# 64-key score blocks in query subgroups of 256, with each chunk's exp split over separate PSUM banks

## The chip, the cores and the metric

The kernel runs on one core of a Trainium2 chip. The metric is the device time of one execution in microseconds (us). A profiled execution also has a span, from its first to its last instruction, which is 1.8 us shorter than the time of the same run (307.76 against 306.0 us before the change). PE is the matmul engine (TensorE) and PEld its weight loads, DVE is VectorE, ACT is ScalarE, POOL is GpSimd.

## The reference, cut to what matters

One transformer block on 2048 tokens of 512 features: adaptive layernorm, sliding-window attention with 32 heads of 16 features, then a token-mixing MLP of width 1792.

```python
mod = (_silu(c) @ w_mod).reshape(c.shape[0], 6, 1, -1)       # six vectors sa, ca, ga, sb, cb, gb
h = _layernorm(x) * (1 + ca) + sa
# attention: 32 heads of 16, window of 256 keys
scores = jnp.einsum('bhqd,bhkd->bhqk', q, k) * Dh ** (-0.5)
mask = (idx[:, None] - idx[None, :] >= 0) & (idx[:, None] - idx[None, :] < 256)
p = _softmax(jnp.where(mask, scores, -1e9))
x = x + ga * (p @ v, heads joined) @ wo
h = _layernorm(x) * (1 + cb) + sb
# MLP over tokens
u = _gelu(jnp.einsum('bsd,sf->bdf', _layernorm(h), w1) + b1)
x = x + gb * (jnp.einsum('bdf,fs->bds', u, w2) + b2)
```

## The kernel before

The 2048 queries go in four groups of 512. Heads go in four sets of eight. Four heads share the PE array by row tiles, and a chunk fills a score tile of four PSUM banks, one bank for each `j`, which one exp reads. The kernel lays out eight PSUM banks: four for the scores (`pss`), one each for value products and sums (`pox`, `poy`), two for everything else (`psd`).

```python
pss = box["s"] = ps_s.tile([P, 4, D], F32, name="pss", tag="pss")      # ps_s has bufs=1
for pi, (kb, q0, nq, at) in enumerate(ch):
    for j in range(4):
        rows = slice(32 * j, 32 * j + 32)
        te.matmul(pss[:, j, HB * at : HB * (at + nq)], lhsT=KT[r][g8][rows, kbi, :, :, :],
                  rhs=QT[G % 2][g8][rows, HB * q0 : HB * (q0 + nq)], start=pi == 0, stop=False, ...)
...
def e_e(e, i=i):
    et_of[i] = epool.tile([P, 4, D], BF, name="et")
    ac.activation(out=et_of[i][:], in_=box["s"][:], func=ACT.Exp, scale=SCORE_SCALE)
```

The chunks called "l" do the half-filled blocks at the window's edges with many small matmuls (64 scores of 32 columns for each of two head sets, four at a time), and DVE multiplies their exps by a mask (`el`). Sums of exps come from a product with a constant `ones_bd`. Their reciprocal is taken on ACT, as `exp(-ln(sum))` (`lz`), and a DVE multiplication writes `OT`. Instructions are issued in a fixed order, kept as a long list of numbers in the source. In it a letter behind a number sends an operation to ACT, DVE or POOL.

The softmax here doesn't subtract the row's maximum and nothing guards it: scores larger than these inputs give would overflow.

Of the kernel before, what the change touches and what calls it, by code (L numbers as in the profile page):

```python
# [10 lines left out]
ALU = mybir.AluOpType  # L11
PSUM = bass.MemoryType.PSUM

P = 128
# [10 lines left out]
HB = 32  # L25
NC = S // NG // HB
# [21 lines left out]
41 30 0 3 42 55 5 49 4 48 13 38 12 54 56 29 1 40 57 78 6 58 2 34 8 37 25 79 53 7 45 15 59 44 80 22 39 9 33 10 81 82  # L48
51 11 46 26 43 83 60 35 20 50 32 16 47 85 84 36 14 61 52 86 28 63 87 18 88 21 89 64 27 90 93 19 92A 91D 94 31 24 96D
95A 17 97 98 100 99A 101 104 102A 103D 105 235 145 107A 112 106D 146 113 115D 108 109 114D 111A 148 62 116 149 110D  # L50
117 123 119D 124 118D 125A 151 152 120 126 121 127 131 122D 132 236 154 133A 134 237 128 155 135 129 238 136 130D
147 163 156 137 164 150 139 157 140 239 166 144 23 153 240 167 138D 158 241 65 242 141D 159 169 66 69 142 170 143 67
70 243 160 175 68 244 176 245 161 73 162 571 403 178 248 179 249 247D 165 246D 168 404 252 251A 250D 181 171 74 182
255 256 253 172 254D 184 173 268 174 185 269 257D 270D 264 259 193 77 177 271D 258 194 186 272 265 196 405 180 197
183 187 273 267D 199 188 200 266D 275D 276 277 274D 189 301 278D 279 302 406 260 261 280 190 304 305 191 281D 192 76
195 263D 283 407 307 262D 198 282 308 292 284 293 294D 310 201 311 285 71 286D 75 202 313 72 203 745 749 295 204 314
748 296 746 752 303 750 205 747 297A 322 315 306 323 206 316 287 288 289A 300 325 207 309 326 408 312 217 291 211
290 572 212 328 409 208 329 410 209 213 317 210 318 218 331 214 332 215 416 216 411 319 337 417 338 320 412 413 418D
321 415D 324 219 414A 340 419D 327 341 220 330 423 333 221 343 420 222 344 424 421 425D 334 422D 346 427 436 347 226
299 428 429 298 437 430D 335 349 223 439A 350 336 438D 339 342 431D 358 224 432 359 345 433 351 447 361 435D 348 362  # L60
353 434D 225 448 354 364 455 449D 365 456 352 440 457D 450 355 367 426 444 368 356 441 451 227 357 458 443D 442A 469
459 228 360 470 363 229 445 573 230 472 366 232 473 231 452 233 369 234 446D 453 370 475 454D 376 371 574 373 476
372 377 575 478 378 374 479 379 380 381 481 375 385 471 482 382 386 383 474 384 490 387 463 491 460 388 483 389 493
464 494 390 461 477 468 576 394 496 480 497 577 485 484 578 486 499 391 500 392 487 505 506 488 393 489 492 465A 395
508 466 495 509 498 396 467 501 397 753 754 502 462D 511 398 512 580 399 402 401 400 579 755 503 514 756 504 515 581
757D 507 583D 584 585 582D 517 587D 586D 591 518 592 596 597 593A 599D 526 510 527 595 598D 588 594 589 600 590D 529
519 513 530 601 608 609 516 603A 610D 532 602D 521 533 611D 612 613 520 758 522 535 614D 523 759 760 536 761 764
762D 765 524 766 637 525 638 528 604 605 640 606D 767 641 607D 531 534 768D 537 643 538 620 644 621 615 622D 616 769
539 617D 646 540 619 770 647 541 618 771 542 772 649 773D 774 543 639 650 553 623 624 547 625D 548 658 549 642 659
651 544 631 545 652 661 632 662 546 645 633D 550 551 554 634 664 552 626 628 665 629 555 627 648 636 763 635 775 556  # L70
630A 667 653 668 776 780 777 654 781 655 673 778 674 656 782 657 660 557 676 779A 558 663 677 783 786 785 784D 787
751 562 788 679 559 666 680 669 791 560 792 789 670 682 790A 561 793 683 797 798 794 799 796 671 685 795A 672 800
686 675 801D 678 563 802 694 564 803 695 808 565 804 809 687 805 566 697 681 806D 698 684 568 689 570 569 688 813
690 700 691 814 815 701 692 810 567 816 811 703 693 704 696 699 702 812A 705 817D 819 706 830 833 820 832 707 821
842 822 835 708 709 818 823D 844 710 836 712 711 713 721 715 716 714 722 717 718 869 729 824 825 875 723 719 733 845
724 846 720 870 734 876 725 826 881 741 726 730 827 828A 829 831 727 887 839 857 840 735 863 728 838 851 807 731 888
736 837 852 834 882 841 742 843 864 737 883 877 732 738 858 889 871 739 847 859 743 740 865 853 744 848 854 849 878
860 850 855 866 856 861 890 884 862 867 872 893 868 873 911 874 879 905 917 885 912 894 886 891 918 880 899 895 892
900 939 901 896 906 897 923 940 898 913 907 908 929 902 914 903 930 924 909 925 910 915 931 919 904 920 932 921 926
933 927 969 949 928 959 916 979 970 922 934 950 989 999 980 1000 981 982 960 961 990 941 962 942 943 971 972 951 944  # L80
991 935 963 936 945 1001 946 952 953 1009 1019 954 955 964 956 1020 1010 937 965 957 938 1029 1021 947 1002 966 948
1011 1030 983 992 1031 993 1003 973 974 1022 1012 994 984 1039 985 975 995 976 1023 1032 967 1040 977 968 1013 1024
986 978 1033 958 1041 996 1014 1004 1005 1034 1006 1042 1035 987 1043 1007 1015 1049 997 1069 1016 998 1050 1008
1070 988 1079 1071 1025 1051 1026 1059 1052 1017 1053 1060 1036 1018 1044 1027 1045 1054 1037 1061 1046 1055 1038
1072 1028 1047 1062 1063 1056 1048 1073 1074 1064 1065 1057 1080 1066 1058 1075 1081 1076 1082 1083 1077 1084 1067
1085 1078 1086 1068 1087 1088
# [3 lines left out]
def run_order(ops):  # L90
    engines = {"A": "ACT", "D": "DVE"}
    left = set(range(len(ops)))
    for word in ORDER.split():
        n = int(word.rstrip("AD"))
        o = ops[n]
        if any(d.n in left for d in o.deps):
            raise RuntimeError(o.name)
        left.discard(n)
        o.emit(engines[word[-1]] if word[-1] in engines else next(iter(o.engs)))
    if left:  # L100
        raise RuntimeError(sorted(left))
# [3 lines left out]
E_BUFS = 5  # L105
WARM = 24



CHUNKS = [  # L110
    [(-1, 0, 7, 0), (-4, 0, 1, 7), (7, 15, 1, 8), (4, 9, 7, 9)],
    [(-2, 0, 5, 0), (5, 11, 5, 5), (-3, 0, 3, 10), (6, 13, 3, 13)],
    [(0, 1, 8, 0), (1, 3, 8, 8)],
    [(2, 5, 8, 0), (3, 7, 8, 8)],
]
CHUNK_G0 = [(7, 15, 1, 0), (4, 9, 7, 1), (6, 13, 1, 8), (5, 11, 5, 9), (6, 14, 2, 14)]

EDGES = [
    ((8, 0, 2), (6, 0, 2)),
    ((5, 8, 1), (4, 8, 1)),  # L120
    ((0, 8, 1), (7, 8, 1)),
    ((0, 8, 1), (7, 8, 1)),
]
EDGES_G0 = ((0, 8, 2), None)
NEG = -32768.0
# [3 lines left out]
def kernel(  # L129
# [73 lines left out]
    edge_w = const.tile([P, 2, 2, 2, HB], BF, name="edge_w")  # L203
    edge_n = const.tile([P, 2, 4, HB], BF, name="edge_n")
    maskl = const.tile([P, 2, HB], BF, name="maskl")
    ones_bd = const.tile([P, 2 * DH], BF, name="ones_bd")
    nc.gpsimd.memset(ones_bd[:], 0.0)
    par_of = const.tile([P, 2], F32, name="par_of")
    nc.gpsimd.memset(par_of[:], 0.0)
    for q in range(4):  # L210
        par = q % 2
        rows = slice(HB * q, HB * q + HB)
        nc.gpsimd.memset(ones_bd[rows, par * DH : (par + 1) * DH], ZSCALE)
        nc.gpsimd.memset(par_of[rows, par : par + 1], 1.0)
    half = const.tile([P, 4], F32, name="half")
    for hf in range(2):
        rows = slice(KB * hf, KB * hf + KB)
        nc.gpsimd.memset(half[rows, 0:1], 1.0 - hf)
        nc.gpsimd.memset(half[rows, 1:2], float(hf))
        nc.gpsimd.memset(half[rows, 2:3], hf - 1.0)  # L220
        nc.gpsimd.memset(half[rows, 3:4], -float(hf))
# [8 lines left out]
    KT = [[kvpool.tile([P, 8, 2, 2, HB], BF, name=f"KT{r}_{g}") for g in range(ND)] for r in range(3)]  # L230
# [9 lines left out]
    ps_s = ctx.enter_context(tc.tile_pool(name="ps_s", bufs=1, space=PSUM))  # L240
    ps_o = ctx.enter_context(tc.tile_pool(name="ps_o", bufs=1, space=PSUM))
# [15 lines left out]
    def emit_masks():  # L257
        tri4 = modw.tile([P, 4, HB], BF, name="tri4")
        tri = modw.tile([P, HB], BF, name="tri")
        po.memset(tri4[:], 1.0)  # L260
        po.affine_select(
            out=tri4[:], in_=tri4[:], pattern=[[HB, 4], [1, HB]],
            compare_op=ALU.is_ge, fill=0.0, base=0, channel_multiplier=-1,
        )
        po.memset(edge_w[:], 0.0)
        for q in range(4):
            rows = slice(HB * q, HB * q + HB)
            po.tensor_copy(out=tri[rows, :], in_=tri4[rows, q, :])
# [51 lines left out]
    def e_warm(e):  # L320
        if "warm" not in box:
            box["warm"] = ps_o.tile([P, D], F32, name="pox")
# [767 lines left out]
```

## Time and profile before

| | before |
|---|---|
| median time | 306.6 us (3 runs), 307.8 us (4 runs, with the profiled one) |
| span | 306.0 us |
| PE busy | 263.4 us, 86% |
| DVE busy | 190.9 us, 62% |
| ACT busy | 178.3 us, 58% |
| POOL busy | 29.3 us, 10% |
| head, to the first exp | 22.1 us |
| attention, to the last value matmul | 193.3 us |
| tail (MLP) | 90.6 us |

A busy share is an average over stages that have different limits, so the table is read by its last three rows. The lines behind them stand in the prediction.

### The profile page before, as it was taken

The page shows a single profiled execution, that of the slowest core. Times are in us where ns is not written, and L with a number is a line of the kernel's source. Part 1 is how long each engine was busy: PE and PEld are TensorE (multiplying, and loading weights), DVE is VectorE, ACT ScalarE, POOL GpSimd, SP SyncE. Part 2 cuts the span into 40 slices and gives each one's busy share as a digit, 9 for nine tenths or more (in the row PEclk, how much of TensorE's full clock was granted, in tenths as well). Part 3 has the DMA queues.
Part 4 walks back from the last instruction along what each step waited for, and adds up shares of the span by engine and source line. Part 5 has one row for each costly group of instructions (what it writes and reads, how often), then busy time and mean ns, then how long its engine had stood idle before and what let it go on. Part 6 is the DMA issues. An engine that isn't in the chain of part 4 may idle for free.

```text
span 306.0 us, 12754 instructions
## 1 busy us (share of the span) xinstructions
PE 263.4 (86%) x5961; PEld 148.4 (49%) x5961; DVE 190.9 (62%) x367; ACT 178.3 (58%) x178; POOL 29.3 (10%) x87
## 2 busy tenths in 40 slices
PE   8287988897988878858899989969999999999973
PEld 3154655554455653545566536446443444444431
DVE  5345997856767886988474682755696531144754
ACT  2057787886788799799597669848342722000000
POOL 8101111010102050001100130000000000000000
PEclk9789999999899999999999999999999999999999
DMA  6997000006900000000000410520689600011121
GB/s 122 243 348 253 5 2 4 4 4 181 237 4 4 4 2 5 4 2 4 4 4 4 111 30 4 140 72 2 250 295 372 257 0 0 0 36 52 61 76 51
DMA packets 31453, 24.94 MB, mean 82 GB/s; under 512 B 6056, under 2 KB 29608, under 8 KB 31400
## 3 DMA queue, kind: packets, MB, share of 16 engines
q1 hardware_dynamic: 30336, 23.08, 25.0%
q10 hardware_dynamic: 1064, 1.05, 1.1%
q8 instruction: 46, 0.75, 1.0%
q14 instruction: 7, 0.06, 0.1%
HBM read 22.03 MB, written 2.10 MB: 79 GB/s over the span
## 4 chain that ended last, share of the span: by engine, by line
PE 66%; ACT 20%; issue 5%; DVE 4%; DMA 3%; SPq 1%; ACTq 0%; DVEq 0%
PE pu L169 32%; ACT et L169 18%; PE pss L169 12%; PE pq L169 7%; PE pox L169 5%; PE poy L169 4%; PE pa L169 3%; DMA x<-in_A_x_dram 3%; PE pv L169 2%; SPq L169 1%; DVE o L169 1%; DVE a L169 1%; PE pt L169 1%; ACT h1T L169 1%; PE ps_b L169 1%
## 5 line engine op out<-in xcount | busy, mean ns | idle before, releaser
L169 ACT ACTIVATE et<-pss 128x2048 bf16<-128x2048 f32 x68 | 127.6, 1876 | 33.3 <-PE pss L169 31.7
L169 PE MATMUL pu<-hb,w1p 128*128 128x512 bf16 x224 | 54.4, 380 | 2.7 <-DVE a L169 1.1
L169 PE MATMUL pu<-guT,w 128*128 128x512 bf16 x224 | 50.0, 379 | 2.5 <-DVE o L169 2.5
L169 PE MATMUL pss<-QT,KT 32*64 32x32 bf16 (+5 forms) x1744 | 35.4, 210 | 14.1 <-ACT et L169 10.1
L169 PEld LDWEIGHTS <-KT 32*64 32x64 bf16 (+1 forms) x1744 | 22.9, 98 | 37.0 <-issue 34.7
L169 POOL TENSOR_SCALAR KT<-kb,mask_par 128x512 bf16<-128x512 bf16 x30 | 21.6, 736 | 153.4 <-DVE kb L169 80.9
L169 PEld LDWEIGHTS <-w 128*128 128x128 bf16 x224 | 21.9, 98 | 29.5 <-issue 3.6
L169 PE MATMUL poy<-et,ones_bd 128*32 128x224 bf16 (+3 forms) x720 | 31.7, 237 | 4.8 <-issue 4.8
L169 PE MATMUL pq<-h1T,wqkv 128*128 128x512 bf16 x128 | 34.9, 393 | 0.9 <-ACT h1T L169 0.3
L169 PE MATMUL pox<-et,VT 128*32 128x224 bf16 (+3 forms) x720 | 32.2, 239 | 2.6 <-issue 1.9
L169 PEld LDWEIGHTS <-VT 128*32 128x32 bf16 x1680 | 28.6, 94 | 12.0 <-issue 8.8
L169 PEld LDWEIGHTS <-w1p 128*128 128x128 bf16 x224 | 20.4, 98 | 27.1 <-issue 5.2
L169 DVE SCALAR_TENSOR_TENSOR o<-pu,b2FM,bc_gb 128x512 f32<-128x512 f32 x16 | 11.9, 748 | 28.0 <-PE pu L169 27.9
L169 DVE BATCH_NORM_STATS2 st<-x 128x6 f32<-128x512 bf16 x32 | 21.7, 678 | 6.2 <-DMA x<-in_A_x_dram 6.1
L169 DVE TENSOR_SCALAR VT<-pv,par_of 128x512 bf16<-128x512 f32 x27 | 18.9, 738 | 9.7 <-PE pv L169 9.7
L169 PEld LDWEIGHTS <-ones_bd 128*32 128x32 bf16 x784 | 19.2, 96 | 6.8 <-issue 6.1
L169 DVE TENSOR_TENSOR OT<-pox,lz 128x512 bf16<-128x512 f32 x16 | 11.0, 687 | 14.9 <-ACT lz L169 10.6
L169 DVE TENSOR_TENSOR el<-et,maskl 128x2048 bf16<-128x2048 bf16 x16 | 19.2, 1209 | 1.7 <-ACT et L169 1.7
L169 PE MATMUL pv<-wqkv,h1T 128*32 128x256 bf16 x512 | 17.5, 274 | 1.6 <-issue 1.3
L169 ACT ACTIVATE rs<-mv,eps_t 128x4 f32<-128x4 f32 (+2 forms) x19 | 5.6, 292 | 22.1 <-DVE mv L169 22.1
L169 PE MATMUL pa<-wod,OT 128*128 128x512 bf16 x64 | 17.4, 388 | 1.1 <-DVE OT L169 0.6
L169 PEld LDWEIGHTS <-wqkv 128*128 128x128 bf16 x128 | 10.5, 100 | 13.1 <-issue 5.1
(82 smaller groups left out, 267.9 us busy)
## 6 DMA issues: line engine op xcount, KB each, us to landing
w1p<-in_B_w_dram SPq DMA_DIRECT2D x14, 512.0 KB, 7.0
w<-in_B_w_dram SPq DMA_DIRECT2D x14, 512.0 KB, 8.1
x<-in_A_x_dram SPq DMA_DIRECT2D x16, 128.0 KB, 5.6
wmod<-in_w_mod_dram SPq DMA_DIRECT2D x4, 512.0 KB, 7.6
out_dram<-otile SPq DMA_DIRECT2D x16, 128.0 KB, 1.7
wmod<-in_w_mod_dram ACTq DMA_DIRECT2D x2, 512.0 KB, 6.2
wqkv<-in_A_wqkv_dram SPq DMA_DIRECT2D x2, 384.0 KB, 5.1
wqkv<-in_A_wqkv_dram SPq DMA_DIRECT2D x1, 512.0 KB, 4.0
```

Source lines behind the costliest of these rows:

```text
L169: ins = call(*args, **kwargs)
```

## The change

The intent is to let exp and scores overlap. The score tile of four banks becomes one of three banks (`psa`) plus two of one bank each (`psb`, two buffers). While ACT works on the `psb` part, PE may refill `psa`. The bank for the second `psb` comes from the sums: with subgroups of 256 queries a value product and its sums are 256 columns each and share one bank (`pxy`). All blocks are now 64 keys wide. The "l" chunks go, and there are 75 chunks in place of 68.

```diff
-                    pss = box["s"] = ps_s.tile([P, 4, D], F32, name="pss", tag="pss")
+                sa = box["sa"] = ps_s.tile([P, 3, D], F32, name="psa", tag="psa")
+                sb = box["sb"] = ps_s.tile([P, D], F32, name="psb", tag="psb", bufs=2)
+                bank = lambda j: sa[:, j, :] if j < 3 else sb[:]
...
-                ac.activation(out=et_of[i][:], in_=box["s"][:], func=ACT.Exp, scale=SCORE_SCALE)
+            def e_ea(e, i=i):
+                et_of[i] = epool.tile([P, 4, D], BF, name="et")
+                ac.activation(out=et_of[i][:, 0:3, :], in_=box["sa"][:], func=ACT.Exp, scale=SCORE_SCALE)
+            def e_eb(e, i=i, own={}):
+                ac.activation(out=et_of[i][:, 3, :], in_=sb_of[i][:], func=ACT.Exp, scale=SCORE_SCALE)
...
-                unit["x"] = ps_o.tile([P, D], F32, name="pox")
-                unit["y"] = ps_o.tile([P, D], F32, name="poy")
+                        unit["xy"] = ps_s.tile([P, 2, KB * QB], F32, name="pxy")
```

With it come other changes. In subgroups 0 to 3 masks are added to the scores on PE, as before; in 4 to 7 DVE multiplies the exps by them. Half of the second-half token sums of the MLP (`p2`) move into attention. In the tail all eight banks serve as homes for products. The first query group is projected in two halves, and the `wmod` loads are issued earlier. Last, many layernorm pieces and the zero fills of `VT` may now go to POOL:

```diff
-    def normalize(dst, src, key, i):
+    def normalize(e, dst, src, key, i):
...
-        ve.tensor_scalar(
+        (ve if e == "DVE" else po).tensor_scalar(
...
+    vt_zero = [op("vz", {"DVE": 1.7, "POOL": 4.3}, lambda e, r=r: (ve if e == "DVE" else po).memset(VT[r][:], 0.0), pos=-20.0 + 5 * r)
+               for r in range(3)]
...
-            xn_ops.append(op("xn", {"DVE": 0.325}, lambda e, i=i: e_xn(e, i), deps=[st[i]] + before + xn_ops[-1:], pos=p_ln + 3.2, sh=True))
+            xn_ops.append(op("xn", {"DVE": 0.325, "POOL": 0.7}, lambda e, i=i: e_xn(e, i), deps=[st[i]] + before + xn_ops[-1:],
+                             pos=p_ln + 3.2 + (i // 2 * 3.0 if G == 0 else 0.0), sh=True))
```

## The prediction

> **What bounds the kernel now.** I read the page first: its engine totals, the 40 slices and the costliest groups.
>
> ```profile
> PE 263.4 (86%) x5961; PEld 148.4 (49%) x5961; DVE 190.9 (62%) x367; ACT 178.3 (58%) x178; POOL 29.3 (10%) x87
> ...
> PE   8287988897988878858899989969999999999973
> ...
> ACT  2057787886788799799597669848342722000000
> ...
> L169 ACT ACTIVATE et<-pss 128x2048 bf16<-128x2048 f32 x68 | 127.6, 1876 | 33.3 <-PE pss L169 31.7
> ```
>
> No engine is full, so the shares do not name the bound. There are three stages: a head to the first exp at 22.1 us, attention from there to the last value matmul at 215.4 us (where ACT is busy), and a tail to 306.0 us (where PE is busy and ACT soon idle). In the group line the 68 exps take 127.6 us, and ACT stood idle 31.7 us before them, waiting for scores. Then the chain of waits, in order of time:
>
> ```profile
> 104.08 0.49 PE pss L169 x24
> 104.60 1.89 ACT et L169
> 106.53 0.49 PE pss L169 x16
> 107.04 1.89 ACT et L169
> 108.97 0.49 PE pss L169 x16
> 109.49 1.89 ACT et L169
> ```
>
> Exp and scores alternate with nothing beside them: a period of 2.44 us of which ACT works 1.88. The timeline shows why:
>
> ```profile
> 106.53 0.40 PE L169 MATMUL pss<-QT,KT 32*128 32x256 bf16 x8 [0.16 <-ACT et L169]
> 106.75 0.24 PE L169 MATMUL pss<-edge_n,edge_w 32*128 32x64 bf16 x8
> 106.92 0.55 PEld L169 LDWEIGHTS <-wqkv 128*128 128x128 bf16 x4
> ...
> 107.04 1.88 ACT L169 ACTIVATE et<-pss 128x2048 bf16<-128x2048 f32 x1
> ...
> 108.82 0.62 ACT L169 ACTIVATE lz<-lz 128x512 f32<-128x512 f32 x1
> ```
>
> The one four-bank score tile is refilled only once the exp has read it (106.48); the scores start at 106.53, occupy PE 0.39 us (to 106.92), and exp starts at 107.04. So a period is 1.88 + 0.05 + 0.39 + 0.12 = 2.44 us. The lz line shows another thing: an instruction that waits for nothing starts 0.10 us before the one ahead ends (107.04 + 1.88 = 108.92), so back to back an exp occupies 1.78 us.
>
> The tail, from the costliest groups and the chain:
>
> ```profile
> L169 PE MATMUL pu<-guT,w 128*128 128x512 bf16 x224 | 50.0, 379 | 2.5 <-DVE o L169 2.5
> 239.52 54.35 PE pu L169 x250
> ```
>
> 250 matmuls in 54.35 us: 0.2174 us each, PE without a gap.
>
> **What the Trainium skill says.** "ScalarE: Activation LUTs", section Rules for kernel authors, gives about 0.3 us per ACTIVATE plus 0.83 ns per element. The trace agrees in slope: 512 columns from PSUM take 592 ns, 2048 take 1876 ns, so 0.836 ns a column; its fixed part is smaller, 592 - 428 = 164 ns. "PSUM — Partial Sum Buffer", section PSUM bank collisions, wants PSUM guarded by bank; that is the reason for refilling only after the read, and why splitting the tile by banks can help. "Perfetto Trace Analysis", section Optimization Strategy, says that the same bubble repeated on the engine that should be full can mean too few buffers; the repeated 0.56 us is that. "TensorE: Matmul & The Clock Gate", on phases on the wall clock, has 216 ns for a warm 512-column matmul; the 0.2174 us agrees.
>
> **The change, part by part.** I counted the instructions of both programs in issue order.
>
> 1) Exp. 68 exps of 2048 columns become 75 of 1536 and 75 of 512: 64-key blocks without the "l" chunks waste more columns. By the line above they last 1.448 and 0.592 us, or back to back 1.35 + 0.495 = 1.84 per chunk against 1.78. The sixteen 512-column ln/reciprocal pairs become 32 of 256 columns: back to back 0.28 + 0.34 against 0.495 + 0.555. In all ACT has 75 x 1.84 + 32 x 0.62 = 158 us here, against 68 x 1.78 + 16 x 1.05 = 138. The change **adds 20 us of ACT work**.
>
> 2) The loop. The 512-column part now runs while PE refills the three banks, so the loop is 1.45 + 0.05 + scores + 0.13. Scores take about 0.22 us (plain, from two to three column blocks) to 0.40 (with mask matmuls), which makes 1.85 to 2.05 us, under ACT's own 1.84 plus the ln or small work that most chunks carry. The bubble goes.
>
> 3) PE. The instruction count falls from 11924 to 9476: 1744 score matmul loads become 960, 1680 value loads become 960. By columns at 2.4 per ns and four tiles at once, with a floor of 0.03 us for a group of four value matmuls, 0.04 for a mask group and 0.06 for a score group, scores fall from 29.2 to 24.7 us and values plus sums from 37.3 to 32.4. The rest of PE is the same.
>
> 4) Steps. For each chunk I set side by side ACT's work up to the next exp, the loop, and PE's work up to the next scores (0.2175 us a 512-column matmul, 0.0272 a pv, 0.11 for a switch between full and tiled), and took the largest. Before: sums over 67 steps ACT 147, loop 167, PE 155; largest each time 179.3. Measured first to last exp: 212.81 - 22.09 = 190.7, so 11.4 are missing. PE's idle "issue" gaps (poy 4.8, pss 2.7, pox 1.9, pv 1.3 in the table of waits) are 10.7. After: over 74 steps ACT 162, loop 145, PE 155; **largest each time 171.5**. ACT binds in 40 steps, PE in 26. Only 8 us better than before, because the loop is replaced at once by ACT's added work.
>
> 5) DVE. Subgroups 4 to 7 get their masks by multiplying on DVE: 32 of 512 columns, 16 of 256, 8 of 1536. From the el group (2048 columns, 1209 ns) I estimate 0.39, 0.25 and 0.92 us, 24 us together against 19 of the old el. With the new part adds and the evacuations, DVE's issue order holds some 85 us in the last 40 chunks, whose steps sum to 90. That is almost full, and it feeds value matmuls and frees PSUM. I allow 11.5 us over the 171.5 for what the steps leave out: about 5 for issue gaps (a fifth fewer PE instructions, none of the dense "l" chunks) and the rest for waits behind DVE. With some 3 us from the last exp's start to the end of its value matmuls, attention takes 171.5 + 11.5 + 3 = **186 us** against 193.3.
>
> 6) Head. The first half of the first group is projected alone, from x tiles 0 and 1, and the wmod loads are issued ahead of an ACT instruction that made them wait until 4.6 us. Before, sT (13.78) stood behind the statistics of an x tile that landed at 12.65. After: wmod about 10.5 to 11, its matmuls 1.0, modFM 0.3, h1T 1.1, eight half-width pq 0.9, copies 0.8, scores 0.5: first exp near **16 us**, not 22.1.
>
> 7) Tail. After the last value matmul PE had 128 pu + 16 pa + 224 = 368 matmuls, 80.0 us of a measured 90.6. Half of the second-half token sums move into attention; the issue order leaves 92 + 8 + 224 = 324, 70.5 us. Eight homes of one bank each also remove the three waits for o (2.5). The end after the last matmul (4.4) stays; layernorm of two last tiles leaves 2 to 3 us of gaps. **77 us**.
>
> Sum: 16 + 186 + 77 = **279 us**; of the 27 gained, 6 are the head, 7 attention, 14 the tail.
>
> **The rivals.** A: ACT alone binds attention, with no losses: 16 + 171.5 + 3 + 76 = 266. For it: 40 steps are ACT's and six exp buffers give slack; against: every stage before lost some 6% to gaps. B: DVE becomes the bound of subgroups 4 to 7, because every mask stands in one queue with the copies that free the two psd banks; each chunk there would take 2.5 in place of 2.25 us, 10 us more: 289. For it: 85 of 90 us; against: DVE's back-to-back instructions overlap a little, so 80 is nearer. C: the single bank of sums and Z stalls the value matmuls, as ln, one exp part, reciprocal and multiply (about 3 us) must pass before the next unit; 32 times 0.5 us would be 16 us: 295. Against: the order places those matmuls in batches some three chunks apart. D: the second MLP product waits for its weights: 7.8 MB after attention took about 27 us for 8.3 MB before (215.5 to 242.5), against 24 us until they are needed: at most 2 us, in the 77.
>
> **Range and chances.** All of A to B within 266 to 289, C partly: range 265 to 292. Nothing I found eats all 27 us. Faster by over 2%: 0.95; within 2%: 0.04; slower: 0.01.
>
> **What would show it right or wrong.** In the profile after: the first psa exp near 16 us; steps of about 2.2 us in the chain, with ACT in a row (psa, psb, lz) and few idle times behind scores, against 31.7 us; ACT over 195 us busy; DVE near 200 and nine tenths in the later slices; the last pxy matmul near 202; then about 77 us. If waits for et masks or OT stand high on PE, B or C was right. It is wrong if PE's cost of many small masks and tiled matmuls is well over my sums, so that PE and not ACT stands in the steps.

## More of the kernel before

Even fast runs of one kernel were granted slightly different TensorE clocks (given as shares of full speed), and their times follow them. Where a per cent matters, I therefore also compare runs of like clock.

## The result, and the profile after

The changed kernel took 284.4 us in the median of 4 runs (281.4 to 284.4) against 307.8 us (305.3 to 309.6) of the kernel before in the same rounds. The ratio is 0.922, with a 95% interval of 0.913 to 0.932. A ratio here compares the fast runs of one kernel with those of the other in the same rounds; it lies within 0.002 of the ratio of their means, and is not quite the ratio of the medians. Repeated, the change came to 285.8 us and 0.928 (0.920 to 0.936).

From the page of the changed kernel: busy time of the engines, then slices of ACT and POOL, then groups. A group line has the count of instructions, the busy time, the mean of one in ns, and the idle time before them with its releaser.

```profile
PE 249.7 (88%) x4693; PEld 140.1 (50%) x4737; DVE 209.7 (74%) x428; ACT 186.5 (66%) x279; POOL 96.1 (34%) x132
...
ACT  2074988999679999995999999899832661000000
POOL 8745790344007559695020041105226000000000
...
L192 ACT ACTIVATE et<-psa 128x1536 bf16<-128x1536 f32 x75 | 109.0, 1453 | 11.5 <-PE psb L192 6.4
...
L192 PE MATMUL pu<-guT,w 128*128 128x512 bf16 x219 | 48.4, 379 | 0.3
L192 ACT ACTIVATE et<-psb 128x512 bf16<-128x512 f32 x75 | 44.8, 598 | 0.0
...
L192 POOL TENSOR_SCALAR xn<-x,mv,rs 128x512 bf16<-128x512 bf16 x14 | 29.2, 2090 | 36.4 <-ACT rs L192 34.3
```

Idle time of ACT before the exps has fallen from 33.3 to 11.5 us, and in the tail the idle time before the `guT` products from 2.5 to 0.3 us. ACT's slices stand at 9 in most of attention. What is new at the bottom is POOL, 96.1 us in place of 29.3. A normalisation takes 2.09 us there.

In the chain of waits in order of time, the bubble of the prediction is gone:

```profile
60.21 1.45 ACT et L192
61.66 0.28 ACT lz L192
61.94 1.85 ACT et L192 x2
63.78 0.30 ACT lz L192
64.09 1.91 ACT et L192 x2
```

From 60.21 to 66.0 us ACT works without a gap: two exp parts and a piece of `lz` in each chunk. In this stretch scores no longer stand between exps. It is the exception in the chain of waits and not the rule: over the whole of attention (190.2 us) the chain runs 86 us through PE, 42 through DVE, 33 through ACT and 19 through POOL. Before the change it was 120 through PE, 58 through ACT, 2 through DVE and none through POOL. By stages:

| | before | predicted | after |
|---|---|---|---|
| head, to the first exp | 22.1 | 16 | 16.8 |
| attention, to the last value matmul | 193.3 | 186 | 190.2 |
| tail | 90.6 | 77 | 75.6 |
| span | 306.0 | 279 | 282.6 |

So 15.0 of the 23.4 us gained are the tail, 5.3 the head and only 3.1 attention, where the main idea lies. Two places in the chain of waits and the timeline of the changed kernel show what attention lost. First the chain, at 18 us:

```profile
18.36 0.92 POOL KT L192 x2
19.28 2.06 POOL xn L192
21.34 0.46 POOL KT L192
21.80 2.07 POOL xn L192
23.91 0.41 PE pt L192 x3
```

For 5.5 us the path runs through POOL, which masks keys (`KT`) and normalises (`xn`) in one queue. Then the timeline, at 37 us (start, duration, engine, operation):

```profile
37.39 3.51 POOL L192 MEMSET VT<- 128x4096 bf16 x1
...
37.98 3.55 DVE L192 TENSOR_SCALAR xn<-x,mv,rs 128x512 bf16<-128x512 bf16 x2
```

Two normalisations on DVE take 3.55 us. One of them took 3.06 us, where the median of that operation is 0.41 us. It ended at 41.04, just after POOL's fill of `VT` (40.90). The Trainium skill, "SBUF — State Buffer", section Who interferes with whom, says that DVE and GpSimd share one pair of memory ports, and that a DVE instruction in a two-port mode contends for it with GpSimd: whichever issues first keeps the pair for its whole instruction while the other blocks. The trace agrees: the fill started first, and the DVE instruction stretched until it was done. Which port mode DVE was in, the trace does not show. Not every DVE instruction is stretched: beside the first fill (30.59 to 34.11 us) copies out of PSUM took their usual 0.42 and 0.69 us, and layernorm statistics 0.69.

The fill is not the only case. Some of DVE's mask multiplications (`et` by `maskt`) were stretched beside POOL's layernorm pieces: one of 256 columns, 0.29 us in the median, took 1.24 from 175.47, and ended at 176.71, just after a POOL multiplication (175.37 to 176.56).

### The profile page after: what moved, and what is told of

The parts are those of the page before. It is cut to its first block, busy times and chain, and to the rows that moved or that the text cites. A ratio compares the mean times of both kernels' runs of the same rounds, so it can differ in the third digit from the quotient of the medians.

```text
span 282.6 us, 10503 instructions
## 1 busy us (share of the span) xinstructions
PE 249.7 (88%) x4693; PEld 140.1 (50%) x4737; DVE 209.7 (74%) x428; ACT 186.5 (66%) x279; POOL 96.1 (34%) x132
## 3 DMA queue, kind: packets, MB, share of 16 engines
q1 hardware_dynamic: 30336, 23.08, 27.1%
## 4 chain that ended last, share of the span: by engine, by line
PE 54%; DVE 18%; ACT 12%; POOL 8%; issue 4%; DMA 3%; POOLq 0%; DVEq 0%
PE pu L192 27%; ACT et L192 9%; PE pxy L192 8%; PE pq L192 6%; PE psa L192 6%; POOL xn L192 4%; DVE VT L192 4%; DVE et L192 3%; PE pa L192 3%; POOL h L192 2%; DMA wmod<-in_w_mod_dram 2%; DVE xn L192 2%; DVE h L192 2%; PE pv L192 2%; ACT lz L192 2%
## 5 line engine op out<-in xcount | busy, mean ns | idle before, releaser
L192 ACT ACTIVATE et<-psa 128x1536 bf16<-128x1536 f32 x75 | 109.0, 1453 | 11.5 <-PE psb L192 6.4
L192 ACT ACTIVATE et<-psb 128x512 bf16<-128x512 f32 x75 | 44.8, 598 | 0.0
L192 PE MATMUL pxy<-et,VT 128*32 128x192 bf16 (+3 forms) x960 | 37.7, 235 | 6.4 <-DVE OT L192 5.5
L192 POOL TENSOR_SCALAR KT<-kb,mask_par 128x512 bf16<-128x512 bf16 (+1 forms) x36 | 23.1, 655 | 56.4 <-DVE kb L192 52.8
L192 POOL TENSOR_SCALAR xn<-x,mv,rs 128x512 bf16<-128x512 bf16 x14 | 29.2, 2090 | 36.4 <-ACT rs L192 34.3
L192 PE MATMUL pxy<-et,ones_bd 128*32 128x192 bf16 (+3 forms) x960 | 37.8, 234 | 0.0
L192 PE MATMUL pq<-h1T,wqkv 128*128 128x512 bf16 (+1 forms) x147 | 33.7, 343 | 2.9 <-DVE VT L192 1.6
L192 PE MATMUL psa<-QT,KT 32*128 32x192 bf16 (+3 forms) x720 | 30.3, 233 | 5.8 <-ACT et L192 4.9
L192 PE MATMUL psb<-QT,KT 32*128 32x192 bf16 (+3 forms) x240 | 29.7, 234 | 0.0
L192 DVE TENSOR_TENSOR et<-et,maskt 128x512 bf16<-128x512 bf16 (+2 forms) x56 | 28.0, 532 | 2.2 <-ACT et L192 2.2
```

The source lines that it names most:

```text
L192: ins = call(*args, **kwargs)
```

## The experiments

My theory after the result was: the overlap works as predicted, and attention lost some 4 us more than predicted to the layernorm pieces and fills on POOL, which the prediction did not count. The rivals: DVE is the bound in subgroups 4 to 7 because of the masks (rival B of the prediction); the single bank of sums and values stalls PE (rival C). All experiments gave correct results. Each ratio is to the kernel before, run on the same chip in the same rounds.

### One buffer for `psb`, and a spare bank for the sums

```diff
-                sb = box["sb"] = ps_s.tile([P, D], F32, name="psb", tag="psb", bufs=2)
+                sb = box["sb"] = ps_s.tile([P, D], F32, name="psb", tag="psb", bufs=1)
```

> The one-bank score tile psb gets one buffer in place of two, nothing else: the scores of a chunk must then wait for the second exp of the chunk before, so the overlap that the split was made for is gone and all else stays. My theory (the split takes the bubble away): the loop becomes 1.45 + 0.50 + 0.05 + scores 0.25 to 0.40 + 0.13, about 2.4 to 2.5 us, and the sum of the largest of ACT, loop and PE over the 74 steps rises from 171.5 to 187.0: about 15 us more, 298 to 301 us. Rival (attention is bound by PE and DVE, the bubble would be hidden): under 4 us more.

It measured 309.2 us (308.2 to 310.4), ratio 1.002 (0.998 to 1.007): as slow as the kernel before. The gains of the head (first exp at 15.7) and of the tail (75.6 us) are still there, and attention, at 215 us, has lost as much. From its page, and then from its chain of waits in order of time:

```profile
L192 ACT ACTIVATE et<-psa 128x1536 bf16<-128x1536 f32 x75 | 108.8, 1450 | 37.0 <-PE psb L192 28.5
```

```profile
86.95 1.44 ACT et L192
88.39 0.19 ACT rs L192
88.61 0.20 ACT rs L192
88.82 0.49 ACT et L192
89.35 0.26 PE psb L192
...
89.90 1.44 ACT et L192
```

ACT is idle 37.0 us before these exps in place of 11.5, most of it behind scores. One turn, from 86.95 to 89.90, is 2.95 us. The second exp must have read `psb` before PE may refill it, and everything that stands between the two exps on ACT (here two `rs`, elsewhere `lz`) now lengthens the loop. In the same chain the turn from 84.43 to 86.95, with nothing in between, takes 2.52 us. My expectation was some 15 us of loss; I had not counted these small pieces, and it was about 24. In the trace the pieces between the two exps of a chunk add up to 8.3 us, about what was missing. So without the second buffer, attention as changed is 22 us longer than before. This is not the price of the block shape alone: split exps, PE's moved sums and POOL's pieces are in it too, and no run has the new blocks without them.

The second run gives the freed bank to `pxy`. It was run at another time.

```diff
-                sb = box["sb"] = ps_s.tile([P, D], F32, name="psb", tag="psb", bufs=2)
+                sb = box["sb"] = ps_s.tile([P, D], F32, name="psb", tag="psb", bufs=1)
...
-                        unit["xy"] = ps_s.tile([P, 2, KB * QB], F32, name="pxy")
+                        unit["xy"] = ps_s.tile([P, 2, KB * QB], F32, name="pxy", bufs=2)
```

> One psb bank (as in psb_single, ratio 1.002) and two banks for sums and Z in place of one. It tests my rival C, that the single bank of sums and Z stalls the value matmuls. C true in size (16 us): ratio 0.950, 292 us. C as the table of waits of the changed kernel has it (5.5 us behind the last multiplication, 4 times): 0.985 at best, 303 to 305 us. No cost, since the matmuls are placed in batches and the scores set the end here: 0.998 to 1.006, 307 to 310 us. The latter is what I expect, and the wait for the multiplication should be gone from the table of waits.

It measured 309.9 us, ratio 1.006 (0.999 to 1.013): no gain over the single bank. The wait of value matmuls for the `OT` multiplication is gone from its table of waits; the changed kernel has it as follows (total, times, longest):

```profile
PE pxy L192 <- DVE OT L192: 5.5, 4, 3.1
```

So where scores set the pace, rival C costs nothing. The changed kernel itself cannot be given a second bank, since its eight banks are all in use; that there too the 5.5 us lie beside other work is an argument and was not measured.

### DVE's masks, the zero fills and the normalisations, one at a time

First, the masks of all subgroups are added on PE, and DVE's 56 multiplications go:

```diff
-            added = u in ADDED
+            added, multiplied = True, u not in ADDED
...
-            m = xb if added else op(f"M{i}", {...}, e_mask, ...)
+            m = xb if not multiplied else op(f"M{i}", {...}, lambda e: None, ...)
```

> Subgroups 4 to 7 get their masks as matmuls added to the scores, as 0 to 3 do; the 56 mask multiplications on DVE (28 us) emit nothing. PE gets 640 small mask matmuls, by my sums 6.4 us. If DVE binds the second half of attention (rival B of the prediction): 3 to 6 us faster, 279 to 281. If PE, 94% busy there, binds: 4 to 7 us slower, 288 to 291. If ACT binds: within 1 us.

It measured 281.8 us (281.4 to 283.5), ratio 0.914 (0.910 to 0.919). At like clock it had 283.5 us at 0.982, against 284.4 of the changed kernel: at most 1 us, which these runs cannot tell from nothing. Though DVE's busy time fell from 209.7 to 185.6 us, its masks were not what attention waited for.

Second, the two fills of `VT` that stood on POOL inside attention go to DVE at earlier places in the issue order (numbers 79 and 80):

```diff
-67 227 79P 318D ... 211 205 80P 148D
+20 62 79D 21 ... 98 140D 80D 189
```

> The two zero fills of value tiles move from POOL (3.51 us each, at 30.6 and 37.4 us) to DVE (1.76 us each) earlier in its order, one in the idle time before modFM and one before the second h1T. During the second fill one DVE xn took 3.06 us in place of 0.41. If that blocking and POOL's own 7 us stand on the path: 1.5 to 3 us faster, 281.5 to 283. If hidden: within 0.7 us. If the fills on DVE delay the head: 1 to 2 us slower.

It measured 282.1 us (281.3 to 283.4), ratio 0.915 (0.910 to 0.919). At like clock: 281.3 us at 0.982 against 284.4, and 282.7 and 283.4 at 0.972 against 284.4 at 0.973. So 1 to 3 us are the fills. The DVE normalisation of 3.06 us is gone; the longest is 0.67 us.

Third, the 18 normalisations that POOL did (`xn`, `n2`, `hb`) go to DVE, at the same places in the order:

```diff
-        o.emit(engines[word[-1]] if word[-1] in engines else next(iter(o.engs)))
+        o.emit("DVE" if word[-1] == "P" and o.name in ("xn", "n2", "hb") else engines[word[-1]] if word[-1] in engines else next(iter(o.engs)))
```

> The layernorm subtractions that the change put on POOL (14 xn, 4 hb; 2.09 us each there, 0.42 on DVE) go to DVE, in the same place of the order; multiplications and additions stay on POOL. If slow POOL normalisation stands on the path (POOL is 8% of the chain that ended last, PE waits 4 us for xn): 3 to 6 us faster, 278 to 281. If DVE, with 7.4 us more, is the bound: 0 to 4 us slower. If both are off the path: within 1 us.

It measured 276.7 us (276.3 to 277.3), ratio 0.898 (0.894 to 0.902). That is faster than the changed kernel by 5 to 7 us (276.3 to 276.5 at 0.988 against 281.4 at 0.991; 277.3 at 0.974 against 284.4 at 0.973). DVE took over 18 instructions, some 7.4 us of work, and is busy just as long as before, 209.7 us. Most of it is made up because its own instructions are held up less: the mean normalisation falls from 578 to 430 ns, the masks of 512, 1536 and 256 columns from 446, 1081 and 429 to 415, 962 and 405 ns, together some 5 us. Not all holding up is gone: two masks still take 1.24 us each beside POOL's multiplications. The chain of waits by engine, of the changed kernel and then of this one:

```profile
PE 54%; DVE 18%; ACT 12%; POOL 8%; issue 4%; DMA 3%; POOLq 0%; DVEq 0%
```

```profile
PE 57%; DVE 20%; ACT 12%; DMA 7%; issue 3%; SPq 1%; DVEq 0%
```

POOL, 8% of the span on the chain, has left it. (The 7% of DMA are the first loads and one load of MLP weights, `w1p`, of 7.8 us at 184 us; waits of PE and PEld for `w1p` are some 2 us in the table of waits.) In place of the run of POOL shown above, its chain at that stage has:

```profile
19.46 0.61 DVE st L192
20.07 0.02 issue
20.09 0.18 DVE mv L192
20.27 0.45 DVE xn L192
20.73 0.03 issue
20.76 0.71 DVE VT L192
```

The same `xn` takes 0.45 us on the path in place of 2.06. The time from the first exp to the last fell from 185.0 to 177.0 us. Most of it, 5.2 of these 8.1 us, is won in the first stretch, from the first exp to the first full-width `h1T` copy of the second group (`h1T` is the normalised input, transposed, that the projections read): 26.2 us in the changed kernel (16.8 to 43.0), 21.0 here (18.1 to 39.1). In this stretch PE was busy 21.1 and 19.6 us at a mean granted clock of 0.93 and 1.00; so 3.7 of the 5.2 us are idle time of PE, and 1.5 us may be the clock.

### Do these gains add?

The changed kernel again, and three variants, on one chip. The first of them is the changed kernel unaltered.

> The changed kernel once more, unaltered, so that the three variants of this call have it on the same chip. Its ratio to the kernel before was 0.922 with an interval of about 0.01 on either side; masks_on_pe and zero_dve came to 0.914 and 0.915 on another chip, and were called faster than the change by 0.008 only across calls. Theory 1 (these two gains are real): the ratio here is again 0.922 or a little below, 0.918 to 0.926. Rival (they were a difference between chips or calls): it comes to 0.913 to 0.916, and then neither the masks on DVE nor the zero fills on GpSimd cost anything that these runs show.

It measured 285.8 us, ratio 0.928 (0.920 to 0.936), so the theory that the two small gains are real stands as far as the ratios go (0.928 is a little above its range); the like-clock comparisons above make that of the masks doubtful.

Next, fills and normalisations both on DVE, by the two edits above:

> Both at once: the layernorm normalisations that stood on GpSimd go to VectorE (norm_dve, ratio 0.898), and the two fills of VT go to VectorE earlier (zero_dve, 0.915). Theory 1: the costs are separate stalls (a VectorE instruction of 3.1 us beside a fill; pieces of 2.1 us of GpSimd on the chain of waits), so the gains add: ratio 0.922 x (0.898/0.922) x (0.915/0.922) = 0.891, about 274.5 us. Rival: both hang on the same thing, GpSimd's share of the time in which VectorE wants the memory, and norm_dve has already taken all of it: 0.897 to 0.899, 276 to 277 us.

It measured 276.0 us (274.7 to 276.4), ratio 0.897 (0.893 to 0.901). My rival holds: the gains do not add. With POOL's normalisations gone, the fills no longer cost anything that shows. From its first exp (16.0) to the last (193.5) it takes 177.5 us.

On top of that, masks on PE for all subgroups, by the first edit:

> The former plus masks added on TensorE for all subgroups (masks_on_pe, ratio 0.914). Theory 1, VectorE is nearly full in subgroups 4 to 7 and the pieces taken over from GpSimd make it fuller, so that taking away its 28 us of masks is worth more than alone (more than 0.008): ratio 0.876 to 0.883, 270 to 272 us. Rival: TensorE becomes the bound there, as the masks are 24 more groups of small matmuls for it, and nothing is won over norm_zero: 0.889 to 0.895, 274 to 276 us.

It measured 278.9 us (278.5 to 279.3), ratio 0.907 (0.903 to 0.911), which is slower by 2.9 us, and it is outside the ranges of both my theories. Busy times from 135 us to the end of attention (last value matmul at 197.7 and 202.1 us; stretch, length, PE, PEld, DVE, ACT, POOL, granted clock, DMA), without and with the masks on PE:

```profile
135.00:197.50 62.50, 61.63 (x1279) 31.87 (x1281) 55.31 (x126) 58.67 (x86) 11.53 (x12) 1.00 0.24 62
```

```profile
135.00:202.00 67.00, 66.64 (x1709) 38.11 (x1708) 40.57 (x85) 60.64 (x88) 10.48 (x12) 1.00 0.23 58
```

PE is busy 61.6 of 62.5 us (99%) already without them. DVE is busy 88% and drops to 61% with nothing won. So once POOL is off the path it is PE, not DVE, that bounds the second half of attention, and rival B falls: had DVE been the bound, this kernel would have been faster.

Last, the multiplications and additions of the second layernorm go to DVE too, while the fills stay on POOL:

```diff
-        o.emit(engines[word[-1]] if word[-1] in engines else next(iter(o.engs)))
+        o.emit("DVE" if word[-1] == "P" and o.name != "vz" else engines[word[-1]] if word[-1] in engines else next(iter(o.engs)))
```

> All pieces of the layernorms, the multiplications and additions too (1.16 to 1.25 us each on GpSimd, 0.42 us on VectorE), go to VectorE; the fills of VT stay on GpSimd. Theory 1, latency of GpSimd on the chain is the cost and VectorE has room: a little better than norm_dve, ratio 0.885 to 0.896, 273 to 276 us. Rival, VectorE becomes the bound: some 14 more pieces of 0.42 us, 6 us, on an engine that is 86% busy after 135 us, so it comes out at 0.900 to 0.910, 277 to 281 us, with waits behind VectorE on the chain.

It measured 276.4 us (273.9 to 278.0), ratio 0.898 (0.891 to 0.905), the same as with the normalisations alone. The pieces of 1.2 us cost nothing measurable where they stood.

### Latency of the results, or POOL being busy?

The normalisations are on DVE as above, but POOL does 18 pieces of the same kind at the old places, on a scratch tile that nobody reads.

```diff
+        if word[-1] == "P" and o.name in ("xn", "n2", "hb"):
+            idle_piece()
...
+    def idle_piece():
+        if not idle_set:
+            idle_set.append(po.memset(idle_t[:], 0.0))
+        po.tensor_scalar(
+            out=idle_t[:], in0=idle_t[:], scalar1=eps_t[:, 0:1], scalar2=eps_t[:, 0:1], op0=ALU.subtract, op1=ALU.mult,
+        )
```

> norm_dve (layernorm normalisations on VectorE, ratio 0.898 on another chip) plus, on GpSimd, 18 pieces of the same kind and size at the places from which they were taken, on a scratch tile that nobody waits for: GpSimd is as busy as in the changed kernel (some 96 us), but its pieces of 2.1 us are on nobody's path by their results. Theory 1, what the change lost to GpSimd is latency, the matmuls waiting for a result that took 2.1 instead of 0.42 us: the ratio stays near norm_dve's, 0.895 to 0.904, 275 to 278 us. Rival, the loss is interference, VectorE being held up while GpSimd works (as one normalisation of 3.1 us beside a fill of VT was): the ratio goes back toward the changed kernel's 0.922 to 0.928, at least 0.914, 282 to 286 us. Some of either: in between, and the share tells how much.

It measured 281.7 us (280.0 to 283.0), ratio 0.915 (0.908 to 0.922), against 0.898 without the pieces and 0.922 to 0.928 for the changed kernel. At like clock: 282.1 and 283.0 us at 0.979 against 283.0 of the changed kernel; 280.0 at 0.994 against 281.4 at 0.991. So most of the loss is back though no result of these pieces is used. Its chain of waits at 18 us:

```profile
18.43 0.94 POOL KT L194 x2
19.36 0.47 POOL idle L194
19.93 2.07 POOL idle L194
22.00 0.46 POOL KT L194
22.46 2.06 POOL idle L194
24.52 0.47 POOL KT L194
```

The key masks that the next scores need stand in POOL's queue behind pieces that nobody needs. At 38 us one DVE normalisation again takes 2.69 us beside the fill, for in this timing the two met again. From the first exp to the first full-width `h1T` it takes 27.1 us (16.7 to 43.8), as in the changed kernel; after that 156.2 us to the last exp against 155.9 without the pieces and 158.8 in the changed kernel. So the first stretch lost by POOL's queue and by the fill that DVE met; the rest, some 3 us, came from waiting for the results themselves, from held-up masks, or is clock. My expectation named only interference as the rival to latency; that the queue of POOL is a third way I saw only in this trace, and the run does not separate queue and fill. The run with only the fills on DVE goes some way: its first stretch is 24.4 us (17.6 to 42.0) against 26.2 in the changed kernel, at the same clock of 0.93 and with the same 21.2 us of PE work. So of the 5.2 us lost there about 1.8 are the fills, up to 1.5 may be clock, and some 2 are left for POOL's normalisations; this is one profiled run of each.

### The tail and the head

All second-half token sums again after attention, as before the change:

```diff
                 def e_p2(e, fc=fc, lo=lo):
+                    return
...
-            g = op("pa", {"DVE": 0.6}, lambda e, fc=fc: ve.tensor_tensor(
-                out=part[fc][:], in0=box["p2", fc][:], in1=part[fc][:], op=ALU.add), deps=[ps[-1]] + part2_ops[-1:], pos=pos)
+            g = op("pa", {"DVE": 0.6}, lambda e: None, deps=[ps[-1]] + part2_ops[-1:], pos=pos)
...
-        ... for sc in (lo, lo + 1)] for lo in (12, 14)],
+        ... for sc in scs] for scs in ((8, 9, 10, 11, 12, 13), (14, 15))],
```

> The changed kernel with the second-half token sums all after attention again, as in the kernel before: p2 and pa emit nothing, and the last products take eight token blocks instead of four. By the issue order 344 matmuls instead of 324 are then in the tail, 20 x 0.2175 = 4.4 us. Theory 1, as in the prediction (the matmuls moved into attention fill time that TensorE would have idled away, as ScalarE sets the pace there): tail 80 us instead of 75.6, attention the same or 1 us less, ratio 0.935 to 0.945, 287 to 290 us. Rival (TensorE is full at the end of attention, 94% after 135 us, so that moving matmuls there wins nothing): attention shorter by what the tail gets longer, ratio within 0.918 to 0.930.

Its three fast runs took 289.4 to 292.3 us (a fourth, 294.5, was slow), ratio 0.945 (0.934 to 0.956). At like clock it is slower than the changed kernel by 5.0 to 5.3 us (289.4 against 284.4 at 0.981 and 0.982; 289.7 against 284.4 at 0.974 and 0.973; 292.3 against 287.1 at 0.965 and 0.966). Attention is as long as in the changed kernel: the first exp starts at 16.9 and the last at 202.3. Busy times from 135 to 205 us of the repeated changed kernel, then of this one:

```profile
135.00:205.00 70.00, 68.06 (x1420) 35.03 (x1413) 58.92 (x134) 66.34 (x96) 14.56 (x14) 0.99 0.21 55
```

```profile
135.00:205.00 70.00, 61.24 (x1345) 32.88 (x1357) 57.59 (x130) 66.23 (x98) 13.67 (x13) 0.99 0.22 55
```

PE is busy 68.1 us there with the moved sums and 61.2 without, and ACT's share is the same, 95%. The moved matmuls filled time in which PE would have been idle, as the prediction had it. The tail of the profiled run is 81.8 us in place of 75.6.

The `wmod` loads behind the first small exp again (numbers 2 and 1 in the order):

```diff
-48 3 0 4 45 2 55 78D 7 1 35 8 39 5 47 6 31 9 82 56 41 81
+48 3 0 4 45 55 78D 7 35 8 39 5 47 6 31 9 82 56 2 1 41 81
```

> The changed kernel with the loads of wmod issued behind the first small exp of the conditioning again, as in the kernel before (there at 4.6 us instead of about 2.5); the rest of the head as changed. The first exp goes from 16.8 to 19 to 20 us. Theory 1, the head is on the path one to one: the time goes up by 2 to 3 us, ratio 0.930 to 0.938. Rival, the gain of the head is eaten by the first subgroups, which wait for projections and loads of their own anyway: the ratio stays within 0.922 to 0.928, and the last exp starts where it did (202 to 204 us).

Its three fast runs took 287.0 to 287.8 us, ratio 0.933 (0.926 to 0.941); at clocks of 0.972 to 0.974 that is 2.5 to 3.4 us more than the changed kernel's 284.4 at 0.973. This is as much as theory 1 gives the head one to one, with the changed kernel's time taken from another call. Its profiled run fell in a slow state (362 us at a clock of 0.65), so its trace is not used and the shift of the first exp is not shown.

## Why the prediction was right or wrong

The span was predicted as 279 us and came to 282.6: 0.8 more in the head, 4.2 more in attention, 1.4 less in the tail. The time was 284.4, for my sum was one of stages, that is of the span, and I had not added the 1.8 us between span and time. The direction and the range held. That the sum came so near is partly luck: a cost that was left out and an allowance that was too large nearly cancelled (step 4).

- **Step 1, ACT's added work: right.** The parts measured 1.453 and 0.598 us against 1.448 and 0.592. ACT was busy 164.8 us from the first exp to the last, with the small statistics and copies beside the 158 us of exps and `lz`.
- **Step 2, the loop: right.** Idle time before the exps fell to 11.5 us. The run with one `psb` shows that this overlap is worth 24 us, as much as the whole change gains. Without it attention takes 215 us against 193.3 before. The rule of the PSUM page is not the reason for refilling after the read, as I wrote: new scores overwrite what the exp has not read yet, so the refill has to wait in any case.
- **Step 3, PE: the difference right, the sizes too small.** Scores kept PE busy 38.8 us before and 36.3 after, values and sums 49.0 and 40.8. The fall is 10.7 us where 9.4 were forecast, but the sums (66.5 and 57.1 us) were some 20 too low. The floors per group of four were estimates; in the trace before, groups repeat every 0.033 us (values of 32 columns) and 0.028 us (masks of 64).
- **Step 4, which engine sets the pace: only in part as forecast.** I had ACT as the largest in 40 of 74 steps and PE in 26, and looked for "ACT in a row". ACT was busy 164.8 of the 185.0 us from first to last exp, so it was idle for 20, and in all 186.5 us, not over 195. The chain of attention is 86 us PE, 42 DVE and 33 ACT. After 135 us PE is busy 94%, ACT 92% and DVE 86%: three engines are near full, and the path changes between them. The largest of three sums has no term for that.
- **Step 4, the sum of steps: the total near, its allowance for the wrong cause.** I had 171.5 us and allowed 11.5 for "issue gaps" and "waits behind DVE". Measured from first exp to last were 185.0 us, 13.5 over. With fills and normalisations on DVE the same programme takes 177.5, only 6.0 over. The 7.5 us between are the layernorm pieces and fills on POOL (5 to 7 us by times at like clock). The prediction has no term for them at all, and without them its allowance would have been 5.5 us too large. It did not ask which of the moved operations became slower, though before the change POOL had no layernorm piece: its largest group was the 30 key masks, 21.6 of its 29.3 us.
- **Step 5, DVE: masks nearly right, bound not reached.** 32 masks took 446 ns, 16 took 429 and 8 took 1081, so 14.3 + 6.9 + 8.6 = 29.8 us against the 24 estimated. Most of the excess is not size: at their medians (416, 285 and 955 ns) they would be 25.5, and the rest are a few that were held up beside POOL's pieces. Yet taking them off DVE won 1 us at most in the changed kernel and lost 2.9 us in the one without POOL's pieces.
- **Step 6, the head: right** within 0.8 us; across the runs quoted the first exp came between 15.7 and 18.3 us, as the weights landed. The delayed loads cost 2.5 to 3.4 us.
- **Step 7, the tail: right.** 75.6 against 77 us. The moved sums are 5 to 6 us of the 15.0 gained (20 matmuls by 0.2175 us would be 4.4). Of the 44 matmuls fewer in the tail, the other 24 come from the issue order; they and the eight homes were not tested apart.
- **Rivals.** A, ACT alone at a span of 266 us, was too good: even without POOL's pieces the span is 272 to 275, with PE full from 135 us on. B and C are refuted as far as the runs reach. D, the weights of the second product, shows no wait in the tail (0.3 us idle before that group).

What would the change have been without the moves to POOL? The run with normalisations on DVE answers it: 276.7 us, ratio 0.898, better than both kernels. This was not the point of the change, and it came from asking where 4 us had gone.

What stays open: how POOL's loss divides after the first stretch; what the new block shape costs by itself; what the projection of the first group in halves wins in the head; and why the granted clock is lower in the early part of the changed kernel (0.93 against 1.00).

## What to carry to other kernels

Splitting a PSUM tile so that one part is double buffered took away a wait that came before 38 of 68 exps; but count what the new shape adds to the engine that then binds, since here 24 us of overlap paid for other changes in attention that cost nearly as much, and the net gain came mostly from moves at both ends. When operations move to another engine, price them there even if that engine looks idle: a queue in which needed small pieces stand behind long ones can be the path at a third of busy time, as POOL's here. When a gain on one engine brings nothing, look at the busy share of the others in that stretch before taking more work off it.

## What the Trainium skill lacked or had wrong

- "GPSIMD Engine Reference", section 3.1 Elementwise — side-by-side cycle accounting, has one measured pair, a 2048-element fp32 addition, 1.96 times as slow as on DVE. For 512 bf16 columns these runs show more: additions and multiplications 1.15 to 1.25 us against 0.42 to 0.43 (2.7 to 2.9 times), and a normalisation with two per-partition operands 2.07 against 0.41 us (5 times). The page's 2.6 cycles for each element of a two-input operation make an estimate of 1.11 us for 512 (at its 1.2 GHz), near the additions, and the key mask, with one per-partition operand and a constant, takes 0.72 to 0.74 us, a little under the page's best case of 769 ns. What it lacks is a figure for the operation with two per-partition operands: its "roughly 2×" would have priced a normalisation at 0.8 us.
- "SBUF — State Buffer", section Who interferes with whom, agrees with what was seen (a DVE instruction of 0.41 us stretched to 3.06 beside a fill of 3.51 us). It does not say that a profile counts the stretch as busy time, so that moving work from POOL to DVE can leave DVE's busy time where it was (209.7 us with 428 and with 446 instructions).
- "ScalarE: Activation LUTs", section Rules for kernel authors: the prediction took its 0.3 us as the price of every ACTIVATE, but the row says that it holds with the bias as a pointer operand. The trace agrees with the row: the small `rs` pieces with such a bias take 0.29 to 0.30 us, those without 0.20. From the two exp parts, which have none, 1453 ns for 1536 columns and 598 ns for 512, the slope is 0.835 ns a column, as the page has it, and the fixed part is 598 - 428 = 170 ns. So nothing is wrong here.
